# Attention with features on partitions, block sums on VectorE, and a planner that fixes the order on five engines

One core of a Trainium2 chip. The metric is the device time of one execution in microseconds (us), as the median over runs. A trace shows the span from the first to the last instruction of one execution; the time of a run is some 1.8 us longer than the span of the same run (272.97 against 271.2 for the kernel before). A run is called slow when it lies more than 1.5% above the fastest one of the same kernel, and fast otherwise; fast runs are compared with fast runs. Each run also lists the clock that TensorE was granted, as a share of full speed.

## The reference

A pre-normed block on x of 2048 positions by 640 features, in bf16. Both branches read the same layer norm.

```python
xn  = layernorm(x)                                  # no affine part
# A: dilated sliding-window attention, 32 heads of 20, window W = 8, step 2
q, k, v = split(xn @ wqkv)                          # wqkv 640 x 1920
idx    = pos[:, None] - 2 * arange(8)[None, :]      # 8 earlier positions
logits = einsum("bhsd,bhswd->bhsw", q, k[idx]) * 20 ** -0.5   # masked where idx < 0
o      = einsum("bhsw,bhswd->bhsd", softmax(logits), v[idx])
A      = o.reshape(B, S, D) @ wo                    # wo 640 x 640
# B: gated block without an activation function
Bout   = ((xn @ w_gate) * (xn @ w_up)) @ w_down     # 640 x 1536, 1536 x 640
return x + A + Bout
```

## The kernel before

Positions go through in four chunks of 512. TensorE (PE) does the projections, gate and up, and both output products. VectorE (DVE) does the attention proper. q and k have features on partitions; v has positions on partitions, is stored to DRAM and gathered back eight times over (`v8`, one copy of a row per offset). The parts that the argument touches:

```python
def product(g=g, j=j):                       # one offset, 128 x 2560
    off = DIL * (JL * g + j)
    pt = apool.tile([P, KT, CS], BF, name="pw", tag="pw", bufs=6)
    nc.vector.tensor_tensor(pt[:], st["qT"][:], st["kT"][:, :, off : off + CS], ALU.mult)

def heads(g=g):                              # sum over a head's features, on PE
    for i in range(KT):                      # KT = 5 blocks of 128 features
        for j in range(JL):                  # JL = 4 offsets, one column tile each
            nc.tensor.matmul(lps[H * j : H * (j + 1), :], lhsT=Ek[:, i, :],
                             rhs=st["pw", g, j][:, i, :], start=(i == 0), stop=(i == KT - 1),
                             tile_position=(0, H * j), skip_group_check=True)
    nc.scalar.activation(st["e"][:, g, :], lps[:], ACT.Exp, scale=scale)
# ... cut
def spread(ttl, need):                       # exps back to positions on partitions
    def emit():
        nc.tensor.matmul(eT[:, 0 : P + H], lhsT=e[:, 0, tcols(ttl)], rhs=selb[:, 0 : P + H], ...)
        nc.tensor.matmul(eT[:, P : 2 * P + H], lhsT=e[:, 1, tcols(ttl)], rhs=selb[:, P : 2 * P + H], ...)
    op(burst, ("eT", c, ttl), emit, 0.2, need, None, ("e", ("a", c, ttl)), 0.7)   # 0.7: slack
# ... cut: normal(), mix() on v8, add(4), add(2), add(1), o stored and transposed by DMA

# chunk 1: normalised x stored to DRAM, read back by a DMA transpose, and planned with it:
later.append((lambda: (load_x(2), load_down()), when(("turned", 1))))   # load_down: wo and w_down
```

The order on PE and DVE is fixed when the program is built, by a loop that simulates two clocks with an assumed duration per operation.

The softmax here doesn't subtract the row's maximum and nothing guards it: scores larger than these inputs give would overflow.

## Time and profile before

| | kernel before |
|---|---|
| three runs given with it | 271.11, 271.48, 285.82 us |
| the profiled run, its span | 272.97 us, 271.2 us |
| busy share PE, DVE, ACT, POOL | 97%, 73%, 38%, 12% |
| moved by DMA | 50.11 MB |

The timelines of SyncE's and GpSimd's DMA issue: the transposing read-back of chunk 1, and the load of w_down.

```profile
30.59 11.10 SPq L312 DMA_TRANSPOSE xnT<-xnD  x1
...
29.98 1.07 POOL L171 DMA_DIRECT2D wd<-in_B_w_down_dram  x1
```

### The profile page before, as it was taken

To read this page: it belongs to the slowest core of one execution; us is meant where nothing else is said; L and a number is where in the kernel's file an instruction comes from. 1 tells how busy PE (TensorE), PEld (TensorE's weight loads), DVE (VectorE), ACT (ScalarE), POOL (GpSimd) and SP (SyncE) were. 2 spreads that over 40 slices of the span, in tenths; PEclk is the share of its full clock that TensorE was granted. 3 is DMA by queue.
4 is the path that set the end of the run, shared out by engine and by line. 5 is a ranking of instruction groups with operands and counts; after the bars stand their busy time and mean duration, and the time that the engine had idled before them with its cause. 6 is when DMAs were issued, how large, how long until landed. Compare 5 with 4: busy or idle time off the path is not lost.

```text
span 271.2 us, 4215 instructions
## 1 busy us (share of the span) xinstructions
PE 262.1 (97%) x1637; PEld 147.4 (54%) x1656; DVE 198.4 (73%) x280; ACT 103.6 (38%) x185; POOL 33.6 (12%) x74
## 2 busy tenths in 40 slices
PE   8899999699999999999999999999999999999995
PEld 8654444244645677544444677644446764445773
DVE  4453983899999978999993899999579859421221
ACT  3655564355655400255555610055551004555000
POOL 1527500200000042200000002120000302000100
PEclk9999999999999999999999999999999999999999
DMA  6999999949996948997660189896004794300111
GB/s 195 276 394 391 244 270 247 358 132 281 296 292 192 202 130 184 295 324 234 152 111 0 47 267 271 229 311 137 0 2 127 214 237 116 83 2 0 48 51 48
DMA packets 49396, 50.11 MB, mean 185 GB/s; under 512 B 20466, under 2 KB 47040, under 8 KB 49376
## 3 DMA queue, kind: packets, MB, share of 16 engines
q1 hardware_dynamic: 44032, 35.72, 50.2%
q0 software_dynamic: 3040, 11.49, 13.5%
q10 hardware_dynamic: 2304, 2.62, 3.0%
q8 instruction: 13, 0.21, 0.3%
q14 instruction: 7, 0.06, 0.1%
HBM read 35.39 MB, written 9.85 MB: 167 GB/s over the span
## 4 chain that ended last, share of the span: by engine, by line
PE 74%; DMA 12%; SPq 5%; DVE 5%; POOL 1%; issue 1%; DVEq 0%; POOLq 0%
PE psf L628 17%; PE psu L579 15%; PE psg L579 14%; PE psqk L368 12%; PE psf L621 7%; DMA x_t<-in_A_x_dram 6%; PE psv L394 6%; SPq L312 4%; DMA xr<-in_A_x_dram 3%; PE lps L450 3%; DMA xnD<-xn 2%; DVE stats L252 2%; POOL rstd L260 1%; DVE xn L282 1%; SPq L106 1%
## 5 line engine op out<-in xcount | busy, mean ns | idle before, releaser
L579 PE MATMUL psu<-xnT,wu 128*128 128x512 bf16 x236 | 59.4, 379 | 0.5 <-DVE osb L635 0.3
L579 PE MATMUL psg<-xnT,wg 128*128 128x512 bf16 x230 | 59.0, 379 | 0.5
L584 ACT CAST gs<-psg 128x512 bf16<-128x512 f32 x48 | 28.1, 586 | 80.7 <-PE psg L579 77.8
L628 PE MATMUL psf<-wd,hT 128*128 128x320 bf16 x384 | 57.7, 299 | 0.0
L439 DVE TENSOR_TENSOR pw<-qT,kT 128x2560 bf16<-128x2560 bf16 x32 | 46.3, 1485 | 2.7 <-ACT kT L374 2.7
L523 DVE TENSOR_TENSOR v<-v,a 128x5120 bf16<-128x5120 bf16 x16 | 45.2, 2823 | 1.0 <-DMA v<-vD 0.6
L628 PEld LDWEIGHTS <-hT 128*128 128x128 bf16 x384 | 37.5, 98 | 14.4
L368 PE MATMUL psqk<-xnT,wqkv 128*128 128x512 bf16 x195 | 44.2, 379 | 0.3
L579 PEld LDWEIGHTS <-wu 128*128 128x128 bf16 x240 | 23.3, 98 | 28.7 <-issue 1.4
L579 PEld LDWEIGHTS <-wg 128*128 128x128 bf16 x240 | 23.2, 98 | 27.4 <-issue 0.8
L584 ACT CAST us<-psu 128x512 bf16<-128x512 f32 x48 | 28.1, 586 | 25.6 <-PE psu L579 25.6
L538 DVE TENSOR_TENSOR v<-v 128x2560 bf16<-128x2560 bf16 (+1 forms) x32 | 36.9, 1153 | 0.4
L589 DVE TENSOR_TENSOR hT<-gs,us 128x512 bf16<-128x512 bf16 x48 | 19.9, 420 | 20.1 <-ACT us L584 19.8
L368 PEld LDWEIGHTS <-wqkv 128*128 128x128 bf16 x200 | 19.3, 98 | 23.2 <-issue 0.8
L635 DVE TENSOR_TENSOR osb<-psf,xr 128x320 bf16<-128x320 f32 x32 | 15.2, 487 | 20.4 <-PE psf L628 16.9
L621 PE MATMUL psf<-wo_perm,oT 128*128 128x320 bf16 x160 | 27.0, 299 | 0.0
L645 POOL DMA_DIRECT2D out_dram<-osb x13 | 7.1, 544 | 144.3 <-DVE osb L635 144.3
L252 DVE BATCH_NORM_STATS2 stats<-x_t 128x6 f32<-128x320 bf16 x32 | 13.6, 468 | 14.0 <-DMA x_t<-in_A_x_dram 14.0
L394 PE MATMUL psv<-wqkv,xnT 128*128 128x320 bf16 x160 | 23.2, 299 | 0.0
L621 PEld LDWEIGHTS <-oT 128*128 128x128 bf16 x160 | 15.5, 98 | 6.4 <-issue 0.4
L394 PEld LDWEIGHTS <-xnT 128*128 128x128 bf16 x160 | 15.4, 98 | 6.5 <-issue 0.4
L400 ACT CAST v_t<-psv 128x320 bf16<-128x320 f32 x32 | 13.6, 425 | 7.5 <-PE psv L394 5.7
(52 smaller groups left out, 132.7 us busy)
## 6 DMA issues: line engine op xcount, KB each, us to landing
v<-vD SPq DMA_DIRECT2D x16, 1280.0 KB, 7.1
x_t<-in_A_x_dram SPq DMA_DIRECT2D x16, 160.0 KB, 3.4
vD<-v_t ACTq DMA_DIRECT2D x16, 160.0 KB, 4.3
xr<-in_A_x_dram POOLq DMA_DIRECT2D x16, 160.0 KB, 3.6
oD<-o SPq DMA_DIRECT2D x16, 160.0 KB, 2.1
out_dram<-osb POOLq DMA_DIRECT2D x13, 160.0 KB, 2.8
wg<-in_B_w_gate_dram POOLq DMA_DIRECT2D x2, 960.0 KB, 11.0
wu<-in_B_w_up_dram POOLq DMA_DIRECT2D x2, 960.0 KB, 13.0
```

Source lines behind the costliest of these rows:

```text
L252: nc.vector.bn_stats(s[:, hf, :], x_t[:, hf * N2 : (hf + 1) * N2])
L368: nc.tensor.matmul(ps[:], lhsT=wqkv[:, i, r * D + j * P : r * D + (j + 1) * P], rhs=st["xnT"][:, i, :], start=(i == 0), stop=(i == KT - 1),)
L394: nc.tensor.matmul(ps[:, 0:N2], lhsT=st["xnT"][:, i, tcols(ttl)], rhs=wqkv[:, i, 2 * D + n0 : 2 * D + n0 + N2], start=(i == 0), stop=(i == ...
L439: nc.vector.tensor_tensor(pt[:], st["qT"][:], st["kT"][:, :, off : off + CS], ALU.mult)
L523: nc.vector.tensor_tensor(v8[:].rearrange("p w (j h) -> p w j h", j=Dh, h=H), v8[:].rearrange("p w (j h) -> p w j h", j=Dh, h=H), st["a16" ...
L538: nc.vector.tensor_tensor(v8[:, 0:k, :], v8[:, 0:k, :], v8[:, k : 2 * k, :], ALU.add)
L579: nc.tensor.matmul(ps[:], lhsT=w[:, i, f * P : (f + 1) * P], rhs=st["xnT"][:, i, :], start=(i == 0), stop=(i == KT - 1),)
L584: nc.scalar.copy(s[:], ps[:])
L589: nc.vector.tensor_tensor(h[:], st["gu", 0, f][:], st["gu", 1, f][:], ALU.mult)
L621: nc.tensor.matmul(ps[:, 0:N2], lhsT=st["oT", ttl][:, i, :], rhs=wo_perm[:, i, n0 : n0 + N2], start=(i == 0), stop=False,)
L628: nc.tensor.matmul(ps[:, 0:N2], lhsT=st["hT", f][:, tcols(ttl)], rhs=wd[:, f, n0 : n0 + N2], start=False, stop=(f == FT - 1),)
L635: nc.vector.tensor_tensor(osb[:, n0 : n0 + N2], ps[:, 0:N2], xr[:, n0 : n0 + N2], ALU.add)
```

## The change

It is a rewrite (a diff of 1388 lines). Its intent: take work off PE, the fullest engine, and drop the large gather of v. The head's 20 features are permuted on the host to 4 partitions x 5 blocks, so DVE can add the five blocks and PE needs one matmul per offset rather than five. v also gets features on partitions, so shifted views of one tile replace the gather; in exchange the exponentials are stored to DRAM and read back repeated over partitions (`A`), and so is the reciprocal of their sum (`R`). Weights arrive in the layout used, the output leaves transposed, and the order of five engines comes from a planner. The core, abridged (`...` and comments stand for what is cut):

```diff
-    nc.vector.tensor_tensor(pt[:], st["qT"][:], st["kT"][:, :, off : off + CS], ALU.mult)
+    nc.vector.tensor_tensor(                      # two offsets at once, 128 x 5120
+        s["pw", n][:, :, :, lo:hi],
+        s["q"][:, None, :, lo:hi].to_broadcast([P, 2, KT, hi - lo]),
+        pairs(s["k"][:, :, off + lo : off + hi], DIL), ALU.mult)
+def fold(c, n):                                   # adds the 5 blocks
+        nc.vector.tensor_tensor(t[:, :, 0:2, :], t[:, :, 0:2, :], t[:, :, 2:4, :], ALU.add)
+        nc.vector.tensor_tensor(t[:, :, 0, :], t[:, :, 0, :], t[:, :, 1, :], ALU.add)
+        nc.vector.tensor_tensor(f[:], t[:, :, 0, :], t[:, :, 4, :], ALU.add)
-    for i in range(KT):
-        for j in range(JL):
-            nc.tensor.matmul(lps[H * j : H * (j + 1), :], lhsT=Ek[:, i, :], rhs=st["pw", g, j][:, i, :], ...)
+    for w in range(JL):
+        nc.tensor.matmul(lps[H * w : H * (w + 1), :], lhsT=heads, rhs=s["f", 2 * g + w // 2][:, w % 2, :], ...)
-    # eT matmuls, v8 gather, a16, mix on v8, add(4), add(2), add(1), o to DRAM and back
+    # e -> DRAM -> A (repeated); sums on PE -> reciprocal -> DRAM -> R
+    nc.vector.tensor_tensor(s["m", n][:], pairs(s["v"][...], DIL), s["A"][...], ALU.mult)   # mix, 4 per chunk
+    nc.vector.tensor_tensor(b[:], a[:], b[:], ALU.add)                                      # adding up, 3 per chunk
+    nc.vector.tensor_tensor(o[:], a[:, 0], a[:, 1], ALU.add)                                # o, then o * R
+    # w_down and wo are loaded when GpSimd has copied one element ("mark") of the first fold:
+    add("pool", ("wd",), gated(wd, wd_in, slice(None), lambda: st[0]["f", 0][:, 0, 0:1]), 1.2, [("pw", 0, 0)], ...)
```

## The prediction

> **What bounds the kernel now.** I began with the page's busy shares and its slices.
>
> ```profile
> span 271.2 us, 4215 instructions
> PE 262.1 (97%) x1637; PEld 147.4 (54%) x1656; DVE 198.4 (73%) x280; ACT 103.6 (38%) x185; POOL 33.6 (12%) x74
> ...
> PE   8899999699999999999999999999999999999995
> ...
> DVE  4453983899999978999993899999579859421221
> ...
> PEclk9999999999999999999999999999999999999999
> ```
>
> PE is busy from end to end at full clock; DVE is dense in the middle and thin in the last quarter. A busy PE need not be a PE at its peak, so I next read the chain that ended last, in order of time, for the rate of streams without a gap, and the timeline of PE for its first projection.
>
> ```profile
> 128.06 1.08 PE psu L579 x5
> 129.14 1.08 PE psg L579 x5
> ...
> 261.71 1.63 PE psf L628 x12
> ...
> 146.63 1.19 PE lps L450 x20
> ```
> ```profile
> 7.72 2.20 PE L394 MATMUL psv<-wqkv,xnT 128*128 128x320 bf16 x15
> ```
>
> Columns: start, duration, what. Five matmuls of 512 columns take 1.08 us, 0.216 each; twelve of 320 take 1.63, 0.136 each; the twenty matmuls of one head sum take 1.19. The program has, counted from its loops: gate and up 480 x 0.216 = 103.7; q and k 200 x 0.216 = 43.2; v 160 x 0.136 = 21.8; the two output products 544 x 0.136 = 74.0; head sums 8 x 1.19 = 9.5; the eT transposes, 16 pairs that together stream 320 columns, 2.2. Sum 254.4 us. Real work begins at 7.72 and the last group of the chain ends at 266.33 + 1.65 = 268.0, which leaves 3.2 us after it. 260.3 us for 254.4 of work: only about 6 us are lost on PE. PE's amount of work is the bound.
>
> For DVE I read the groups with shapes kept apart:
>
> ```profile
> L439 DVE TENSOR_TENSOR pw<-qT,kT 128x2560 bf16<-128x2560 bf16 x32 | 46.3, 1485 | 2.7 <-ACT kT L374 2.7
> L523 DVE TENSOR_TENSOR v<-v,a 128x5120 bf16<-128x5120 bf16 x16 | 45.2, 2823 | 1.0 <-DMA v<-vD 0.6
> L538 DVE TENSOR_TENSOR v<-v 128x1280 bf16<-128x1280 bf16 x16 | 13.1, 821 | 0.3
> L589 DVE TENSOR_TENSOR hT<-gs,us 128x512 bf16<-128x512 bf16 x48 | 19.9, 420 | 20.1 <-ACT us L584 19.8
> L635 DVE TENSOR_TENSOR osb<-psf,xr 128x320 bf16<-128x320 f32 x32 | 15.2, 487 | 20.4 <-PE psf L628 16.9
> L505 DVE RECIPROCAL rs<-eT 128x32 f32<-128x32 f32 x16 | 5.6, 352 | 5.9 <-PE eT L485 5.7
> ```
>
> They fit one line: elements / 1920 per us + 0.155 us for bf16, and about 1.04 ns per element + 0.155 us for the f32 read from PSUM. The 20 MB gather of v rows cost DVE 0.6 us of waiting in all, so taking it away gains nothing directly.
>
> **What the Trainium skill says.** "TensorE: Matmul & The Clock Gate", Part 1, gives a warm matmul N / 2.4 GHz + about 2.5 ns; that is 0.216 and 0.136 us, as this trace has it. "VectorE: DVE Perf Modes", Mode 2x_1P: a bf16 tensor_tensor with unit step does two elements a cycle at 0.96 GHz, and its errata section adds a fixed cost per instruction; the fit above is both. So splitting an operation costs 0.155 us a piece, and no new layout can beat 1920 per us. "TensorEngine Tiling (Array Packing)", Key Properties: column tiles run in parallel; twenty 32-column matmuls in 1.19 us are five groups of four at 0.238, so it agrees. The first page's specification table also says that the queue of VectorE is strict FIFO; the effect is what rival 1 is about.
>
> **The change, part by part.** It is a rewrite. Weights and constants arrive already laid out, q, k and v are all kept with features on partitions, and the output leaves transposed.
>
> PE. Features are ordered so that a head's 20 features are 4 partitions x 5 blocks; DVE adds the 5 blocks (line 402 on) and the head sum needs one matmul per offset, not five: 160 become 32, 8 groups of four x 0.24 = 1.9, not 9.5. eT goes; the softmax sums are 64 matmuls of 128 columns, four at a time: 16 x 0.056 = 0.9 for 2.2. V and the output products run at 512 columns: 100 + 340 matmuls, 21.6 + 73.4 for 21.8 + 74.0, nothing gained. New sum: 103.7 + 64.8 + 73.4 + 1.9 + 0.9 = 244.7, so 9.7 us less than before.
>
> DVE, per chunk of 512 positions. Products 4 x 2.82 = 11.3 (two offsets each; before 8 x 1.485 = 11.9). Folds, new: 1.22 + 0.69 + 0.69 = 2.60, x4 = 10.4. One reciprocal of 128 elements: (352 - 132 for one element) / 31 = 7.1 ns each gives 1.03. Mix 4 x 2.82 = 11.3; adding up 3 x 2.82 = 8.5, and o 2 x 1.485 = 3.0. Subtotal 45.4. Gates 12 x 0.42 = 5.0, statistics 4.6, residuals 5 x 0.69 = 3.4. 58.5 x 4, + 2.3 for the first chunk's scaling and mask = 236 us, against 198. The trade is therefore 10 us off PE for 38 more on DVE, which had 73 idle. ACT takes over the scaling of chunks 1 to 3 and stays near 107 us.
>
> Where it lies. Start: x0 landed at 3.1 before. In the new DVE order the second tile's scaling stands behind the third tile's statistics, so I put the first projection at 8.7. q and k (100 matmuls of 256 columns, 10.8) and the transposes among them (0.6) end at 20.1, copied at 20.6, where before DVE's first product started at 26.72.
> PE floor: 8.7 + 0.6 + 244.7 + 3.5 (after the last matmul) = 257.5.
> DVE floor: the two instruction orders meet where an output product needs the finished o of its chunk. Before the end of o(2), DVE has from its first product 181.8 (four attentions at 45.4) - 22.7 (mix, adds and o of chunk 3, which come later) + 42 gates 17.6 + two statistics 9.2 + 10 residuals 6.9 + mask 0.2 = 193.0, so o(2) ends at 213.6 at the earliest. PE then still has 188 matmuls of 512 columns (5 + 68 of chunk 2's output, 30 of gate/up, 85 of the last chunk's output) = 40.6, and 3.5 after: 257.7. From o(2) to o(3) DVE has 28.7, inside PE's 35.2, so o(3) isn't the limit.
> Sooner joints, from the same orders: o(0) at 107.4 against PE's arrival at 110.3; o(1) at 159.3 against 160.6; o(2) 213.6 against 213.1. Both engines are critical at once. I add 4 us for stalls (before, PE lost 6 with a less loaded DVE): **262.0 us**, 3.5% faster.
>
> **The rivals.**
> 1. DVE becomes the bound and drags PE. For: the two floors differ by 0.2 us; both queues run in a fixed order made with assumed durations, and the assumed ones are too short against this trace (a fold 2.3 for my 2.60, product and mix 2.75 for 2.82), about 2 us per chunk, so DVE comes late to every joint, PE waits, and later gates wait for PE in turn. Against: the gates are spread thin, and the measured groups have hardly any idle time between dependent instructions. If all 8 us land on the path: 266 to 269, near the border of 2%.
> 2. The round trip of the exponentials. They are stored to DRAM and read back repeated over partitions (128 KB, then 512 KB each); before, issue to landing took 2.1 us for a 160 KB store, 5.4 for 640 KB. Mix(0) has only 6 to 7 us of other DVE work to hide it; in later chunks a whole set of products lies between. A late one adds 1 to 3 us, once or twice.
> 3. PE alone counts and everything else hides: 257.5 to 259. Against: joints with under 3 us of slack.
> 4. Loading. Traffic falls from 50 MB to about 26 (worked out from tensor sizes), but the first 20 us want x, wqkv and the first of wgu together, some 4 to 5 MB at the 350 GB/s that the trace shows there; late v or gate weights would add 1 to 4 us to PE.
>
> **Range and chances.** Under 257.5 needs a start sooner than I think; over 268.5 needs rival 1 whole, or several of the others together. 80%: 257.5 to 268.5. Faster by over 2% means below 266.05: 0.83. Within 2%: 0.16. Slower would need a DVE operation to fall out of its two-per-cycle rate through the new access patterns (shifted pairs, repeated operands): 0.01, as both patterns exist in the measured kernel at full rate.
>
> **What would show it.** In the changed profile: head sums near 2 us and PE's stream about 245 in five-matmul groups of 1.08; DVE busy 230 to 240 and over 88% of the span; the fold's three instructions at 1.22, 0.69, 0.69; the product at 2.82; first product near 20.6; and the ends of o(0), o(1), o(2) near 107 to 111, 159 to 164, 214 to 218. Rival 1 shows as PE waiting for DVE o before the output product (line 607) by several us per chunk; rival 2 as DVE waiting for DMA before line 505; rival 4 as PE idle before 30 us. I am wrong if the folds or shifted products run slower than the fit, or if PE's idle time beyond 10 us has another cause than these.

## More of the kernel before

The page, busy time, chain and groups are read in the prediction; more things are needed later. First, two lines of its page: the DMA total, and the shares of the chain of work that ended last.

```profile
DMA packets 49396, 50.11 MB, mean 185 GB/s; under 512 B 20466, under 2 KB 47040, under 8 KB 49376
...
PE 74%; DMA 12%; SPq 5%; DVE 5%; POOL 1%; issue 1%; DVEq 0%; POOLq 0%
```

Second, the timeline of PE (start, duration, instruction; in brackets the idle time before it and what ended it). These two are nearly all the waiting PE does once the projections have begun.

```profile
10.92 0.45 PE L293 MATMUL pst<-selb,xn_t 128*128 128x128 bf16 x5 [0.99 <-DVE xn_t L282]
...
52.75 0.24 PE L481 MATMUL eT<-selb,e 128*128 128x160 bf16 x1 [2.51 <-DVE e L473]
```

## The result

| | before | after |
|---|---|---|
| all runs | 270.98 to 293.17, 15 runs | 261.27 to 261.77, 12 runs |
| median | 279.68 (fast ones near 271.2) | 261.56 |
| span of the profiled run | 271.2 | 259.8 |
| first projection, last matmul's end | 7.72, 268.0 | 8.85, 256.3 |

The ratio of fast runs is 0.9631 (95%: 0.9612 to 0.965). Here and below, a ratio is the mean time of one kernel's fast runs over that of the other's of the same rounds, so not quite the ratio of the medians quoted. All twelve runs of the changed kernel were fast ones. Of the fifteen of before only five were, with a mean of 271.6, so the ratio rests on these five, and the record labels the comparison "unclear". In the rounds of e2b, on chip 4, before has 21 fast runs with a mean of 271.6.

The page of the changed kernel, in the order of the lines shown of before:

```profile
span 259.8 us, 3385 instructions
...
PE 252.3 (97%) x1293; PEld 121.0 (47%) x1316; DVE 223.2 (86%) x231; ACT 110.5 (43%) x197; POOL 40.3 (16%) x72
...
PE   8799999999999999999999999999999999999994
...
DVE  4646999789999949999999999999999999998014
...
DMA packets 16656, 27.11 MB, mean 104 GB/s; under 512 B 9632, under 2 KB 12448, under 8 KB 16256
...
PE 95%; DMA 2%; DVE 1%; issue 1%; SPq 0%; ACT 0%; DVEq 0%
```

PE is busy throughout, and the chain that ended last is now PE for 95% of the span, where it was 74%. DMA traffic nearly halved. The waits of PE (total, times, longest) show how little is left:

```profile
PE pst L267 <- DVE x_c L244: 1.3, 2, 1.0
...
PE ps L331 <- issue: 0.3, 2, 0.2
```

The first is in the warm-up, ahead of the first projection. Behind that, PE waits 0.3 us in 247.5. The timeline of PE, at the start and around a head sum:

```profile
8.85 0.71 PE L331 MATMUL ps<-xnT,wqkv 128*128 128x256 bf16 x5 [0.33 <-ACT xnT L275]
...
34.35 1.24 PE L569 MATMUL psg<-xnT,wgu 128*128 128x512 bf16 x5
35.52 0.40 PE L417 MATMUL lps<-f,sel 128*32 128x512 bf16 x4
35.85 1.25 PE L569 MATMUL psu<-xnT,wgu 128*128 128x512 bf16 x5
```

Five gate matmuls take 1.08 us of the stream, so without the head sum the next group would have started at 34.35 + 1.08 = 35.43. It started at 35.85: a head sum costs 0.42.

DVE's groups with shapes kept apart (busy, mean ns | idle before it, releaser):

```profile
L391 DVE TENSOR_TENSOR pw<-q,k 128x5120 bf16<-128x5120 bf16 x16 | 45.1, 2819 | 6.8 <-ACT k L352 5.8 <-ACT q L352 0.9
...
L402 DVE TENSOR_TENSOR pw<-pw 128x2048 bf16<-128x2048 bf16 x16 | 19.5, 1222 | 0.1
...
L405 DVE TENSOR_TENSOR f<-pw 128x1024 bf16<-128x1024 bf16 x16 | 11.1, 692 | 0.5
...
L474 DVE RECIPROCAL rs<-sps 128x128 bf16<-128x128 f32 x4 | 3.8, 943 | 1.5 <-PE sps L462 1.5
```

And the timelines of DVE and of PE where the third chunk's attention result o is finished and used:

```profile
210.76 1.49 DVE L524 TENSOR_TENSOR o<-o,R 128x2560 bf16<-128x2560 bf16 x1
212.16 0.75 DVE L589 TENSOR_TENSOR hT<-gs,us 128x512 bf16<-128x512 bf16 x2
212.84 2.82 DVE L505 TENSOR_TENSOR m<-v,A 128x5120 bf16<-128x5120 bf16 x1
...
215.59 1.24 PE L607 MATMUL psf<-o,wo 128*128 128x512 bf16 x5
```

o ends at 212.25, PE comes for it 3.3 us later. Note also the starts: 212.16 is 0.09 ahead of the end of the instruction before, and two instructions of 0.42 together take 0.75. Neighbours on DVE that do not depend on each other overlap.

**Where the time came from**, from the two traces (spans):

| part | before | after | difference |
|---|---|---|---|
| up to the first projection | 7.72 | 8.85 | +1.1 |
| PE's stream less its waits | 256.5 | 247.2 | -9.3 |
| PE's waits in the stream | 3.8 | 0.3 | -3.5 |
| after the last matmul | 3.2 | 3.5 | +0.3 |
| span | 271.2 | 259.8 | -11.4 |

The stream's work is its length (260.3, 247.5) less the waits that the timelines name. PE's work is the main part. The profiled run of before was 272.97, some 1.5 above its typical fast run, so against fast runs (271.6 to 261.5) the gain is nearer 10 than 11.4, and the waits' part of it is worth less than the table says.

### The profile page after: what moved, and what is told of

It reads as the page before. It is cut to its first block, busy times and chain, and to the rows that moved or that the text cites.

```text
span 259.8 us, 3385 instructions
## 1 busy us (share of the span) xinstructions
PE 252.3 (97%) x1293; PEld 121.0 (47%) x1316; DVE 223.2 (86%) x231; ACT 110.5 (43%) x197; POOL 40.3 (16%) x72
## 2 busy tenths in 40 slices
DMA packets 16656, 27.11 MB, mean 104 GB/s; under 512 B 9632, under 2 KB 12448, under 8 KB 16256
## 4 chain that ended last, share of the span: by engine, by line
PE 95%; DMA 2%; DVE 1%; issue 1%; SPq 0%; ACT 0%; DVEq 0%
PE ps L331 25%; PE psg L569 20%; PE psu L569 20%; PE psf L602 20%; PE psf L607 8%; DMA x_c<-x 2%; PE lps L417 1%; PE pst L267 0%; PE sps L462 0%; DVE stats L207 0%; SPq L143 0%; ACT xnT L275 0%; DVE x_c L244 0%; DVE osb L621 0%; DVEq L699 0%
## 5 line engine op out<-in xcount | busy, mean ns | idle before, releaser
L569 PEld LDWEIGHTS <-wgu 128*128 128x128 bf16 x480 | 46.5, 98 | 56.5 <-issue 1.3
L331 PE MATMUL ps<-xnT,wqkv 128*128 128x512 bf16 (+1 forms) x343 | 66.5, 348 | 0.9 <-ACT xnT L275 0.3
L569 PE MATMUL psg<-xnT,wgu 128*128 128x512 bf16 x238 | 59.6, 379 | 0.2
L569 PE MATMUL psu<-xnT,wgu 128*128 128x512 bf16 x234 | 59.0, 379 | 0.3
L602 PE MATMUL psf<-hT,wd 128*128 128x512 bf16 x235 | 54.1, 379 | 0.3
L391 DVE TENSOR_TENSOR pw<-q,k 128x5120 bf16<-128x5120 bf16 x16 | 45.1, 2819 | 6.8 <-ACT k L352 5.8
L505 DVE TENSOR_TENSOR m<-v,A 128x5120 bf16<-128x5120 bf16 x16 | 45.1, 2820 | 0.1
L602 PEld LDWEIGHTS <-wd 128*128 128x128 bf16 x240 | 23.5, 98 | 28.3
L515 DVE TENSOR_TENSOR m<-m 128x5120 bf16<-128x5120 bf16 x12 | 33.7, 2804 | 0.0
L607 PE MATMUL psf<-o,wo 128*128 128x512 bf16 x97 | 24.0, 379 | 0.2
```

Source lines behind the costliest of these rows:

```text
L331: nc.tensor.matmul(ps[:, 0 : hi - lo], lhsT=wqkv[:, b, i, :], rhs=s["xnT"][:, i, lo:hi], start=(i == 0), stop=(i == KT - 1),)
L391: nc.vector.tensor_tensor(s["pw", n][:, :, :, lo:hi], s["q"][:, None, :, lo:hi].to_broadcast([P, 2, KT, hi - lo]), pairs(s["k"][:, :, off ...
L505: nc.vector.tensor_tensor(s["m", n][:], pairs(s["v"][:, :, off : off + CS], DIL), s["A"][:, 2 * n : 2 * n + 2, None, :].to_broadcast([P, 2 ...
L515: nc.vector.tensor_tensor(b[:], a[:], b[:], ALU.add)
L569: nc.tensor.matmul(ps[:], lhsT=wgu[:, f, r, i, :], rhs=st[c]["xnT"][:, i, :], start=(i == 0), stop=(i == KT - 1))
L602: nc.tensor.matmul(ps[:], lhsT=wd[:, f, m * P : (m + 1) * P], rhs=st[c]["h", f][:], start=(f == 0), stop=False)
```

## The experiments

Theory: PE's amount of work bounds the kernel, and the work that DVE gained is hidden. Rival A: DVE and PE are both critical, and DVE work costs time one for one. Rival B: the halved traffic, or the round trip of the exponentials, counts. All times are compared with 261.56 for the change, and for variants of before with its fast runs. A joint is a place where PE needs something that DVE must have finished, such as the attention result o of a chunk. The runs come from three chips (0, 4 and 13), on which the fast runs of before begin at 270.46, 270.52 and 271.43; the changed kernel itself was not run again beside its variants. A difference of less than about 1 us from 261.56 is therefore not a safe one.

### e1_heads5: the head sums' matmuls back to five per offset, DVE's work kept

```diff
-            for w in range(JL):
+            for w in [w for _ in range(KT) for w in range(JL)]:
```

> The changed kernel with every head-sum matmul issued five times over (the count of the kernel before, 160 for 32); DVE's work and the result stay the same. Adds 128 matmuls at 1.19/20 = 0.0595 us = 7.6 us to PE. Theory (PE's amount of work sets the time, the saved matmuls are the gain): 261.6 + 7.6 = 269.2 us. Rival A (DVE, or joints with DVE, set the time): about 261.6 to 263. Rival B (the gain came from the lighter DMA traffic or the earlier start): about 261.6.

Correct; 268.31, 268.53 and 268.68. The 32 extra groups of four cost 7.0 us, 0.22 each, all in full: PE's work is the bound. A fourth run, the profiled one, took 558.65 with every matmul at half its rate (mean 674 to 678 ns against 379), while its record gives a granted clock of 1.0. It is left out, and unexplained, and it shows that a recorded clock alone does not tell a slow run.

### b1_heads1: the kernel before with one of its five head-sum matmuls (wrong result)

```diff
-                    for i in range(KT):
+                    for i in range(1):
-                                start=(i == 0), stop=(i == KT - 1),
+                                start=(i == 0), stop=True,
```

> The kernel before, with only the first of the five accumulating matmuls of each head sum (result wrong on purpose): PE -128 matmuls = -7.6 us, DVE and traffic unchanged. Theory (PE's work bounds the kernel before as well, and the head sums are the larger part of the gain): 271.3 - 7.6 = 263.7 us in fast runs. If traffic, the start or DVE explain the gain, it stays at 270 to 271.

267.12 to 268.98, all fast, mean 267.9; before on the same chip and state 270.46 to 272.90, mean 271.6. So 3.7 us, where the trace of PE shows a group down from 1.26 to 0.40, 6.9 over eight. Part of the rest is visible in the timeline of PE: the wait at 50 us stays (2.78 us, now), and the five matmuls behind it take 2.34 us rather than 1.24.

```profile
51.26 2.34 PE L579 MATMUL psg<-xnT,wg 128*128 128x512 bf16 x5
```

PE runs at a reduced clock after this wait: the granted clock from 51.0 to 53.4 us is 0.50, where in the trace of before it is 1.00 behind the wait of 2.51. The Trainium skill describes the effect in "TensorE: Matmul & The Clock Gate", Part 1: an idle window of about 3.4 us drops PE to half its clock until it has been busy about as long. The drop to half agrees with the trace; the length does not, for here a wait of 2.78 us was enough. It is no accident of the profiled run: the four runs list granted clocks of 0.987 to 0.994, the five fast ones of before 0.998 to 1.0. That is 0.8% of 268 us, so by my estimate some 2 of the missing 3.2 us are the clock. Less PE work alone, in an order made for more of it, therefore gives about half of its worth, since the wait that this order leaves costs the clock as well; the new order is part of the gain. How much each part gives can't be read off more exactly, since the two orders share nothing.

### e2_nofold: two of the fold's three additions removed (wrong result)

```diff
-            nc.vector.tensor_tensor(t[:, :, 0:2, :], t[:, :, 0:2, :], t[:, :, 2:4, :], ALU.add)
-            nc.vector.tensor_tensor(t[:, :, 0, :], t[:, :, 0, :], t[:, :, 1, :], ALU.add)
```

> The changed kernel without two of the three adds of each fold (only one block pair is added, so the result is wrong on purpose). Takes 16 x (1.22 + 0.69) = 30.6 us off DVE and nothing off PE. Theory (PE): 261.6, within 0.7 us; the added DVE work is hidden whole. Rival A (DVE or the joints set the time): faster by several us, 255 to 259, with smaller idle time of PE.

Slower, against every theory: 266.52 to 277.75 (the two fast runs 266.52 and 268.93), with 28 us less of DVE work. Its timelines of SyncE, GpSimd and PE, and its PE clock by stretch (length, busy and matmuls, granted clock, DMA share, GB/s); the profiled run was a slow one, so the sizes are those of a slow run:

```profile
27.55 17.42 SPq L293 DMA_TRANSPOSE xnT<-xnD  x1
...
28.07 0.53 POOL L188 DMA_DIRECT2D wd<-wd  x1
...
50.06 9.03 PE L331 MATMUL ps<-xnT,wqkv 128*128 128x512 bf16 x34 [9.79 <-DMA xnT<-xnD]
...
50.06:53.05 2.99, 2.99 (x7) 0.55 0.00 0
```

The same places in the changed kernel:

```profile
27.45 3.87 SPq L293 DMA_TRANSPOSE xnT<-xnD  x1
...
27.21 2.77 POOL L182 COPY mark<-f 128x1 bf16<-128x1 bf16 x1 [8.51 <-DVE f L405]
29.92 0.53 POOL L188 DMA_DIRECT2D wd<-wd  x1
```

The shorter fold frees the "mark" copy 1.9 us sooner, and with it the 1.9 MB load of w_down. That load then comes 0.5 us after the start of the DMA transpose of chunk 1, no longer 2.5 us after, and the transpose takes 17.4 us to issue where it took 3.9. PE waits 9.79 for it and goes on at about half clock (0.55) for 3 us. The mark itself is one element per partition, and its copy took 2.77 us beside a DVE product: the Trainium skill, "SBUF — State Buffer", in "SBUF: two separate sides", says that a DVE instruction with two SBUF inputs and a GpSimd instruction that reads SBUF lock each other out for a whole instruction. The traces agree: the copy ends 0.04 us behind the product in the changed kernel (29.98 and 29.94), and in e9_start_gate below, where it starts beside a DVE gate of only 0.42 us, it ends 0.04 us behind that gate (32.54 and 32.50), after 0.24. At 0.24 the load would have been issued at about 27.5 us (my estimate), together with the transpose. So it seems that only this lock kept the two transfers apart in the changed kernel; no run takes the lock away.

The experiment changed two things at once. e2b_nofold_late repairs that.

### e2b_nofold_late: the same, with the first fold left whole

```diff
-            nc.vector.tensor_tensor(t[:, :, 0:2, :], t[:, :, 0:2, :], t[:, :, 2:4, :], ALU.add)
-            nc.vector.tensor_tensor(t[:, :, 0, :], t[:, :, 0, :], t[:, :, 1, :], ALU.add)
+            if (c, n) == (0, 0): nc.vector.tensor_tensor(t[:, :, 0:2, :], t[:, :, 0:2, :], t[:, :, 2:4, :], ALU.add)
+            if (c, n) == (0, 0): nc.vector.tensor_tensor(t[:, :, 0, :], t[:, :, 0, :], t[:, :, 1, :], ALU.add)
```

> As the run without two of the three adds of each fold, except that the first fold stays whole. In that run the first fold ended 1.9 us sooner, the load of wd is released by that fold, was issued at 28.07 instead of 29.92 us and got in front of the DMA transpose of xnT(1), which then took 17.4 us to issue instead of 3.9; PE waited 9.8 us for it and came back at a reduced clock. If that explains the slow result, wd is now issued at about 29.9 again, PE has no wait of more than 1 us, and 29 us less DVE work gives 261.6, within 0.7 us (PE is the bound). If the missing DVE work itself disturbs the schedule, it stays at 265 or more. If DVE was the bound, below 260.

261.08 to 261.52, median 261.21, all fast. From its page:

```profile
PE 252.2 (97%) x1293; PEld 120.8 (47%) x1316; DVE 197.0 (76%) x201; ACT 110.5 (43%) x197; POOL 39.6 (15%) x72
```

DVE works 26 us less and the time moves by 0.35. These additions are hidden entirely; rival A falls for the kernel as it is. And e2's loss was the collision: with the load 2.5 us behind the transpose again (27.27 and 29.75), the transpose takes 4.0 us to issue, and PE has no wait of over 0.6 us behind its warm-up.

### e3_fold_plus: one more addition per fold, result unread

```diff
+            nc.vector.tensor_tensor(t[:, :, 2, :], t[:, :, 1, :], t[:, :, 3, :], ALU.add)
```

> The changed kernel with one more add of 1024 elements per fold, written to a part of the tile that nobody reads; result unchanged. DVE +16 x 0.69 = 11 us, order of instructions unchanged. In the trace o(0), o(1), o(2) end 0.9, 1.9 and 3.3 us before PE wants them, and DVE idles 8 us before o(0), of which the waits in the middle absorb some of the delay. Theory (PE is the bound but DVE is only a few us behind it at each joint): +2 to +4 us, 263.5 to 265.5, with PE waiting for o at line 608 or so. If DVE had real slack: 261.6. If DVE set the time already: +11, 272.

Correct; 267.11 to 268.29, median 267.44: 5.9 us for 11 of added DVE work, over the 2 to 4 that I expected. The waits of PE in its trace:

```profile
PE psu L570 <- ACT gs L576: 1.7, 1, 1.7
PE lps L418 <- DVE f L406: 1.5, 2, 1.1
...
PE sps L463 <- DVE e L432: 0.8, 1, 0.8
```

No wait is at an output product for o, where I had placed the joints. PE waits for the folds, for the masked exponentials, and for a copy of ScalarE. By the pages DVE is 8.2 us busier (231.4 for 223.2), since neighbours overlap; 5.9 of these show. So DVE is hidden with only some 2 us of busy time to spare (5 us of instruction durations), and past that it costs.

### e4_replan: e3 with the planner told of the longer fold

```diff
+            nc.vector.tensor_tensor(t[:, :, 2, :], t[:, :, 1, :], t[:, :, 3, :], ALU.add)
-            add("dve", ("pw", c, n), fold(c, n), 2.3, ...)
+            add("dve", ("pw", c, n), fold(c, n), 2.9, ...)
```

> The run with one more add per fold (267.4 us), with the duration that the planner assumes for a fold raised from 2.3 to 2.9, so that the order of instructions is made anew for it; the work is the same. If the 5.9 us came from joints at fixed places in the order (PE waited for mask, statistics and folds that came late), a new order wins back most: 262 to 264.5. If they came from DVE being full, 266 to 268.

Correct; 266.50, 266.52, 266.70 and 270.00. A planner that knows of the work recovers 0.8 of 5.9 us; the waits only move (1.4 for a copy of v, 1.3 for chunk 1's transpose, 1.2 for o). So e3 had not merely upset the order; DVE was near its limit. For fold durations of 2.8, 3.0 and 3.2 the planner ends in its own assertion, without a task that is ready, so nothing finer was tried.

### e5_traffic and e5b_traffic_later: 16 or 12 copies of 1.3 MB from DRAM to DRAM

```diff
+    junkD = dram.tile([16, S // 2, D], BF, name="junkD")
             # in mix(c, n):
+            nc.gpsimd.dma_start(out=junkD[4 * c + n], in_=x[0 : S // 2, :])               # e5
+            if c > 0: nc.gpsimd.dma_start(out=junkD[4 * c + n], in_=x[0 : S // 2, :])     # e5b
```

> The changed kernel with 16 extra copies of 1.3 MB from DRAM to DRAM on the GpSimd queue, one at each mix: 21 MB more moved (21 read, 21 written), about what the gather of v moved in the kernel before. Result unchanged. Theory (PE's work): 261.6 to 262.5, a little for later loads. Rival (the lighter traffic is what made the change faster): 266 to 271.

> As the run with extra DRAM copies, but only from chunk 1 on (12 of the 16 copies, 16 MB). In that run all of the loss but one ACT wait of 0.9 us followed one event: two copies were issued at 51.6 and 52.4 us, just before the first read-back of exponentials, whose mix then waited 6.0 us for DMA; PE waited 2.8 us for the fold behind it. If the traffic hurts only there, this run gives 261.6 to 262.3. If traffic as such costs time, it loses three quarters of 6.7 us: 266 to 267.

Both correct. e5: 267.69 to 268.84, median 268.31, 6.7 us slower. One event stands out in the waits of DVE of its trace (total, times, longest):

```profile
DVE m L507 <- DMA A<-eD: 6.0, 1, 6.0
```

The first chunk's exponentials come back late, and the mix of chunk 0 has little other DVE work around it; a fold behind it comes late for PE (2.8 us). e5b leaves the first chunk alone: 261.45 to 262.43, median 261.56. From chunk 1 on, sixteen MB of further traffic cost nothing. So less traffic is not what made the later chunks faster. In chunk 0 traffic costs time through the round trip of the exponentials, which the kernel before does not have, and which is a weak place there alone. That the saved traffic gave nothing in the kernel before is likely by this, and not shown: e5b has only 576 packets more than the change (17232 for 16656), where before has 49396, and many small packets were not tried.

### e6_start: the statistics of tiles 2 and 3 put behind the scaling of tile 1

```diff
-        add("dve", ("stats", 0, k), stats(0, (k,)), 1.1, [("x", 0, min(k, 2))], ...)
+        add("dve", ("stats", 0, k), stats(0, (k,)), 1.1, [("x", 0, min(k, 2))] + ([("xn", 0, 1)] if k >= 2 else []), ...)
```

> The changed kernel with the statistics of tiles 2 and 3 put behind the scaling of tile 1 on DVE, which in the trace waited from about 5.6 to 7.1 us for them. The first projection should begin at about 7.9 instead of 8.85 us. PE's stream has no gaps after that, so if PE's work is the bound the whole moves: 261.6 - 0.9 = 260.7. If DVE or joints later hold it, 261.4 to 261.6.

Correct; fast runs 260.34, 260.40, 260.53 and 260.63, and two slow ones (264.72, 268.53). The first projection starts at 7.68 rather than 8.85, and the fast runs gain 1.1 on average: the later start of the change seems worth its full length (1.17), as far as a comparison over chips can say. In its profiled run, a slow one, the transpose of chunk 1 took 7.92 us to issue, with the w_down load 0.5 us behind its start. The collision again.

### e9_start_gate: e6, and w_down and wo released by the second fold

```diff
+            if (c, n) == (0, 1): gated(wd, wd_in, slice(None), lambda: f[:, 0, 0:1])(); gated(wo, wo_in, slice(None))()
```

(with the `wd` and `wo` tasks of the plan emptied, so that the order stays that of e6)

> The run with the earlier start, plus the load of wd and wo released by the second fold instead of the first (about 5.7 us later); order of the other instructions unchanged. In two of six executions of the earlier start a reduced clock showed (264.7 and 268.5 us), and its profiled one has PE waiting 2.7 us for the DMA transpose of xnT(1)[...]. If that collision is the cause, here all executions lie at 260.3 to 260.8, PE has no wait over 1 us, and the transpose is issued in under 5 us. If not, some executions stay above 262.

Correct; 260.59 to 261.04, median 260.86, six runs, all fast. Timelines of SyncE and GpSimd:

```profile
28.32 2.83 SPq L293 DMA_TRANSPOSE xnT<-xnD  x1
...
32.76 0.53 POOL L188 DMA_DIRECT2D wd<-wd  x1 [0.22 <-issue]
```

The load now comes 4.4 us behind the transpose, and no slow run was seen. This version beats both kernels: 0.7 us less than the change. It ran on another chip than e6, so the 0.3 us between its runs and e6's fast ones is not explained.

### b2_slack: the kernel before, planned with 4.0 us of slack ahead of the first eT

```diff
-            op(burst, ("eT", c, ttl), emit, 0.2, need, None, ("e", ("a", c, ttl)), 0.7)
+            op(burst, ("eT", c, ttl), emit, 0.2, need, None, ("e", ("a", c, ttl)), 4.0 if c == ttl == 0 else 0.7)
```

> The kernel before with only the assumed delay of its first eT transpose set from 0.7 to 4.0 us, which puts three or four gate and up groups in front of it on PE. In its trace PE waits there 2.5 us at 50 us for the mask of chunk 0. Theory (this wait, and a reduced clock behind it in some executions, is part of what the kernel before loses): fast runs 271.3 - 2.5 = 268.8, and fewer or no runs above 275. If the slow executions have another cause, they stay as frequent.

Correct; 22 runs, the 13 fast ones 270.39 to 271.87, nine slow ones 278.77 to 293.39. The wait of 2.5 us is gone from its trace, but 0.9 us came in its place (eT waiting for `a`), and the fast runs gain 0.2% (ratio 0.9983). So that wait was not worth its 2.5 us, and it isn't the cause of the slow runs. My expectation fell on both counts.

### b3_down_later: the kernel before, w_down and wo held back by a copy of the first exponentials

```diff
+    mark = const.tile([P, 1], BF, name="mark")
+    def gate_down():
+        nc.gpsimd.tensor_copy(mark[:], state[0]["e"][:, 0, 0:1])
+        load_down()
-    later.append((lambda: (load_x(2), load_down()), when(("turned", 1))))
+    later.append((lambda: load_x(2), when(("turned", 1)))); later.append((gate_down, when(("exp", 0, 0))))
```

> The kernel before with its load of wo and wd held back until the first exponentials of chunk 0 exist (about 37 instead of 28 us). In its trace the DMA transpose of xnT(1) takes 11.1 us to issue from 30.6 us on, next to that load. If late transposes with PE idle behind them are what makes a good third of its executions 275 to 293 us long, such executions disappear and the fast ones stay at 270.5 to 272. If the slow ones have another cause, they stay about as frequent.

Correct; 17 runs, median 271.23, highest 275.16. The kernel before had, in the same rounds, 271.43 to 293.02 in 22 runs, 12 of them slow. Timelines of SyncE and GpSimd:

```profile
30.34 2.62 SPq L318 DMA_TRANSPOSE xnT<-xnD  x1
...
39.90 1.07 POOL L177 DMA_DIRECT2D wd<-in_B_w_down_dram  x1
```

The transpose takes 2.6 us to issue instead of 11.1, and the executions above 276 us are gone. The best times stay at 271 (270.87, and 271.43 for before; the ratio of fast runs is 0.9935, as before's fast runs of these rounds reach up to 275.43). So the scatter of the kernel before came from this collision, and the gain of the change doesn't: its 3.7% is between fast runs. What PE waits for in a slow run of before was not seen, as none was profiled; that the collision is the cause rests on its removal. That the changed kernel does not scatter is a second benefit, and it hangs on the 2.5 us by which one load comes later.

## Why the prediction was right or wrong

**The total** came out at 261.56 for 262.0, but by luck: the sum has errors in it that cancel, so I take it apart.

**PE's work: right.** Predicted 9.7 us less, measured 9.3 (256.5 to 247.2); e1 shows that it counts in full. Two terms were too small. Eight head sums were put at 8 x 0.24 = 1.9 and cost 8 x 0.42 = 3.4: I had spread the entry and exit of a long run over its groups. A further group in the same place costs 0.22 (e1), so going over to these tiles and back costs some 0.20 each time; before's twenty matmuls, at 0.42 + 4 x 0.22 = 1.30, agree (33.45 + 1.08 to 35.82, 1.29). The softmax sums were counted as 64 matmuls; there are 32, in four groups, and a group takes 0.32 to 0.56 (two of them with a wait of 0.16 inside), not 0.22. Together they are about the 1.9 us between my 245.3 (244.7 and 0.6 of transposes) and the measured 247.2.

**The start: right.** 8.85 for 8.7; e6 agrees with its price.

**The stalls: the term that was mis-sized.** "I add 4 us for stalls (before, PE lost 6 with a less loaded DVE)". Of the 6, 3.8 were waits and the rest work that my counts lacked. In the changed kernel PE waits 0.3 us, so of the 4 added, 2.2 are there: 1.9 of uncounted work and 0.3 of waits. 257.5 + 2.2 = 259.7, and the span is 259.8, the start being 0.15 later.

**Span and run time: left out.** My sum was one of spans, and I gave it as the time of a run, 1.8 us longer. 259.8 + 1.8 is the measured time; the oversized stall term and this omission hid each other.

**DVE: the failed step is "Both engines are critical at once".** Every duration was close: product 2.82, mix 2.82, folds 1.22, 0.69, 0.69, reciprocal 0.94 for 1.03; DVE's instruction durations add up to 236.1, as predicted. But busy time is their union, 223.2 or 86%, outside the 230 to 240 and over 88% that I had named as a sign, since neighbours that do not depend on each other overlap by 0.08 to 0.09 us; such an operation adds about 0.07 to the stream beyond its elements, not 0.155. Up to the end of o(2) I had 193.0 us of work; DVE was busy 182.5 in that stretch (21.54 to 212.25), and the 8 us of waiting that it also did had room. For the same reason "38 more on DVE" was 25: I compared a sum of durations with a union. The trace of before showed the overlap already, as products of 1.485 that come in pairs of 2.90. o ends at 110.9 and 160.7, inside the ranges given, and at 212.25, sooner than its 214 to 218. PE came for it at 111.7, 162.6 and 215.6, so the joints had 0.8, 1.9 and 3.3 us of slack, and DVE was never critical there; e2b shows that 26 us less of DVE gives nothing. (The prediction's own PE floor puts PE at o(2) at 257.5 - 3.5 - 40.6 = 213.4, where it writes 213.1; this changes nothing.)

**Rival 1 (DVE drags PE): did not happen,** though it stands only some 2 us of DVE busy time away (e3), and then through folds and the masked exponentials, not through o. Its argument that the planner's assumed 2.75 us for a product or mix is too short was mostly wrong: it is the distance from one start to the next where the next instruction is independent (in the trace of DVE the mix at 212.84 is followed by a gate at 215.57, 2.73 later). It is short only where a product's own fold comes next (21.54 to 24.40, 2.86). The fold's 2.3 is short, for 2.7.

**Rival 2 (round trip): did not happen;** no mix waited for DMA, and e5 and e5b place its weakness in chunk 0. **Rival 3 (PE alone counts): is what happened,** at 259.8 of span for its 257.5 to 259 (261.56 as the time of a run), the two mis-sized PE terms and the offset making the difference. I gave it too little weight. **Rival 4 (loading): not at the start,** but the one load I had not looked at, w_down beside a DMA transpose, was the worst hazard in both kernels. No term of the prediction deals with the scatter of before, so it did not foresee that the median over all runs would fall by 18 us (279.68 to 261.56), some 8 of them because the scatter ends.

## What to carry to other kernels

Add DVE up by start-to-start distances read from neighbours in a trace, not by durations, before calling it a second bound; and state whether a sum is a span or a run time. Work moved from a full engine to one with idle time pays its whole worth only if the order leaves slack, so test it from both sides: less of the hidden work must give nothing, and more of it shows how far the next bound is. Look at what a faster step sets free: here a fold that ends 2 us sooner released a load beside a DMA transpose and cost more than it saved.

## What the Trainium skill lacked or had wrong

- "TensorEngine Tiling (Array Packing)", Key Properties, says that changing the tiling mode drains TensorE and gives no size. Here a group of four 32-column matmuls of 512 costs 0.42 us between full-array matmuls, and each further group in the same place 0.22 (e1): some 0.20 us for going over and back.
- "VectorE: DVE Perf Modes", "The DRAIN you can't avoid", says that a semaphore after each operation costs nothing extra. Here independent neighbours overlap by 0.08 to 0.09 us (two of 0.42 in 0.75), and dependent ones stand 0.03 to 0.04 us apart (product from 21.54 for 2.82, its fold at 24.40), so an operation that needs the one before it starts some 0.12 us later than one that does not. Whether the semaphore makes the difference, no run separates.
- "DMA: Bandwidth & Descriptors", "Rules for kernel authors", says that a transpose next to ordinary DMAs needs nothing. That is about correctness, and no result was wrong here but those made so on purpose; for time it does not hold: with a 1.9 MB load issued between 1.6 us before and 0.5 us after its start (before, b1, b2, e2, e6), the transpose took 7.9 to 17.4 us to issue, and 2.6 to 4.1 where the load came 2.4 us later or more (the change, e2b, e3, e4, e5, e5b, e9, b3).
- "TensorE: Matmul & The Clock Gate", Part 1, puts the idle window that halves the clock at about 3.4 us. Here waits of 2.78 us (b1), 2.70 (e6) and 2.83 (e5) were followed by a granted clock of 0.50, and one of 2.51 (before) was not.
